# An S4D scan gated by an MLP: kernel tables through DRAM, outer products placed at once

## The chip, the core and the metric

The kernel runs on one core of one Trainium2 chip. The core has five engines with queues of their own: TensorE (matmuls; PE in the profile, its weight loads PEld), VectorE (DVE), ScalarE (ACT), GpSimd (POOL) and SyncE (SP), which here only issues DMAs. The metric is device time in microseconds: the median of three timed runs, and for the profile the span of one execution from its first to its last instruction.

## The reference

The input `A_u` is one sequence of 2048 tokens with 576 channels. It is layer-normalised, and the result goes two ways: through a long convolution per channel (S4D) and through an MLP whose SiLU gates the convolution.

```python
def _A_ref(u, log_A_real, A_imag, C_real, C_imag, log_dt, D_skip):
    ...
    P = jnp.exp((A * dt[:, None])[:, :, None] * pos[None, None, :])
    K = 2.0 * jnp.einsum("dn,dnl->dl", C, P).real
    ...
    Kf = jnp.fft.rfft(K, L2)
    Uf = jnp.fft.rfft(u_t, L2)
    y = jnp.fft.irfft(Uf * Kf[None, :, :], L2)[:, :, :L]
    ...
    return y + u * D_skip[None, None, :]

def _B_ref(x, w1, b1, w2, b2):
    y = _layernorm(x, axis=-1)
    h = _gelu(jnp.einsum("bsd,df->bsf", y, w1) + b1)
    return jnp.einsum("bsf,fd->bsd", h, w2) + b2

x = A_u
xn = _layernorm(x, axis=-1)
s = _A_ref(xn, ...)
g = _silu(_B_ref(xn, ...))
return x + s * g
```

The state size N is 128, the hidden size 4608. The result is float32.

## The kernel before

**The MLP** is cut into 48 slots: two halves of the tokens, 12 groups of 384 hidden units in each, and two blocks of 512 tokens (`tb`) in each group. A slot has 11 positions: three units of the first layer (14 matmuls of 512 columns each, line 633) and eight units of the second (72 matmuls of 288 columns in all, line 707). Every float32 operand is split into a high and a low part, and three products of these parts are summed. ScalarE applies the GELU (671) and takes the high part (674), VectorE takes the low part (677) and adds the second layer's result (717). Weights are loaded into `raw` by SyncE (551, 553) and split by ScalarE (586) and VectorE (583).

**The tables and outer products.** The convolution kernel of 16 channels (a block `b`, 36 of them) is a product of two small tables of complex powers. `tables(b)` makes them: `load_par` (944) fetches 30 numbers per channel and state, on GpSimd's queue, into one of two `par` buffers; VectorE makes the phases (963, 966, 972), ScalarE the integer parts and the sines (969, 975, 980, 982); VectorE makes the magnitudes `mg` (988) and the four products with the sines (997 to 1003). `kgen(b)` is the outer product: 64 small matmuls (1042), after which ScalarE copies the result into a tile `kt` (1047), one tile for 48 channels, two buffers.

**The chunks.** The convolution itself is a Fourier transform in two stages, made by matmuls, for six chunks of 96 channels. A chunk's steps on TensorE are X1 (1157, two, the signal's first stage), K1 (1188, two, the kernel's), S2 (1217, four, second stage of both), the inverse (1260, two) and I1 (1286, one). Between them ScalarE and VectorE split operands (1133, 1136), transpose (1165, 1196, 1271), multiply (1234) and add (1240). The matrix of the first stage, `f1t`, is split anew for each chunk (1111, 1114) into the buffer of the second stage's matrix, `f2t`.

**What sets the order.** A planner written in Python (`Order`) walks through the 48 slots with assumed durations and writes each engine's instructions in one fixed order. It keeps a clock per engine, a number of lines of steps (each line in order, lines earlier in its list first where two could start at once), and marks for what is done. MLP work is urgent and has due times; the rest fills what is left. DMA loads are steps without an engine, written into their queue when their conditions are met by the plan. After each position of a slot `pe_turns` may put a step of a chunk or an outer product between the MLP's matmuls; at 7 of the 11 positions chunk steps and outer products are allowed. `END` sets the pace of the chunk steps, `ALONE` how long a ready outer product waits for one. `ride` lets an outer product that is ready go inside a chunk step's place, using a free part of its accumulator. All chunk steps take both `cv` accumulators, an outer product alone takes one. `HOLD` moves some named VectorE steps behind the next one on their engine.

The second half's MLP inputs are stored to `y_s`, and before slot 24 loaded (486), transposed (491) and split (495 to 503) through the `row` buffers, of which there are four. The result is put together by `combine` (746 to 758, three `row` buffers per set) and, for the last eight token blocks, by `finish` (802 to 826).

Of the kernel before, what the change touches and what calls it, by code (L numbers as in the profile page):

```python
# [18 lines left out]
P = 128  # L19
# [9 lines left out]
E1, E8, E64, E512 = 2, 10, 18, 26  # L29
NPAR = 30  # L30
PK = 144
NXC, NROW = 1, 4
G = 3
NG = F // (P * G)
KB = 4
# [12 lines left out]
def pool(n):  # L48
    return 0.25 + 0.0023 * n

# [174 lines left out]
def mixer_kernel(ctx, tc, u, log_a_real, a_imag, c_real, c_imag, log_dt, d_skip, w1, b1, w2, b2,  # L225
# [24 lines left out]
    par_s = dr.tile([P, D, NPAR], F32, name="par_s")  # L250

# [13 lines left out]
    f1t = sb.tile([P, 2, 2, 64], F32, name="f1t")  # L265
# [34 lines left out]
    def odd_rows(part):  # L300
# [14 lines left out]
        if part == 1:  # L315
            for g in range(4):
# [86 lines left out]
    def norms(b0, n):  # L403
# [49 lines left out]
        def second(t):  # L453
            mv, rs = MV[b0]
            y = sb.tile([P, D], F32, name="row", bufs=NROW)
# [333 lines left out]
    def finish(b, c0, c1, silu, second_queue, z=None, store=(0, 0), flush=False,  # L789
# [7 lines left out]
        def act_z():  # L797
            if n < D:
                T.append(sb.tile([P, TB], F32, name="h32", bufs=2)[:, :n])
            else:  # L800
                T.append(sb.tile([P, D], F32, name="row", bufs=NROW))
# [33 lines left out]
    def params():  # L835
# [9 lines left out]
        PRM = [flat(sb.tile([P, 12, 64], F32, name="kt", bufs=2)) for _ in range(2)]  # L845
# [57 lines left out]
        add("DVE", d, lambda: V.scalar_tensor_tensor(cr, cr, 2.0, dt, op0=OP.mult, op1=OP.mult), mark="polar")  # L903
        early.append(step("DVE", d, lambda: V.tensor_mul(nrm, nrm, dt), need=["nrm"]))
# [5 lines left out]
        def pack(i):  # L910
            s = slice(i * PK, (i + 1) * PK)

            def columns():
                if i == 0:
                    V.memset(pt[:, :, E1:E1 + 17:8], 1.0)
                V.tensor_copy(pt[:, :, 0], th[:, s])
                V.tensor_copy(pt[:, :, 1], ph[:, s])
# [11 lines left out]
            early.append(step("DVE", 0.6 if i else 1.1, columns, need=["polar"]))  # L929
# [7 lines left out]
    PAR, TAB = {}, {}  # L937

    def load_par(b):
        if b == NB:  # L940
            return
# [11 lines left out]
    def tables(b):  # L953
# [5 lines left out]
        def phase(k):  # L959
            if k == 0:  # L960
                T["v"] = table_tile()
                T["w"] = T["v"][:, :, :, 32:]
                nc.vector.tensor_mul(T["w"][:, 1], bc(PAR[b][:, :, 0], 2, NV), bc(tv, 1, SB))
            else:
                u = T["w"][:, 1, :, 33:]
                nc.vector.tensor_add(u, u, bc(PAR[b][:, :, 1], 2, 32))
# [24 lines left out]
        def weigh(part):  # L991
# [10 lines left out]
            else:  # L1002
# [5 lines left out]
        return ([step(None, 10.0 if b < 6 else 4.5, lambda: load_par(b), mark=("par", b), need=[("pack", b * SB // PK)]  # L1008
                      + ([("mags", b - 2)] if b > 1 else [("xn", k) for k in range(8, NT)])),
                 step("DVE", dve(SB * NV), f(phase, 0), need=[("kg", b - 2)] if b > 1 else []),  # L1010
                 step("DVE", dve(n), f(phase, 1), hold=HOLD.get(("phase", b), 0)), step("ACT", act(SB * NV), whole),
                 step("DVE", dve(SB * NV), frac, hold=HOLD.get(("frac", b), 0)), step("ACT", act(SB * NV), fold, mark=("fold", b))],
                [step("ACT", act(SB * NV), f(sin, 0), need=[("fold", b)], mark=("sin", b, 0), tbl="sin"),
                 step("ACT", act(SB * NV), f(sin, 1), mark=("sin", b, 1), tbl="sin")],
                [step("DVE", dve(2 * n), f(mags, 0), need=[("par", b)]),
                 step("DVE", dve(n), f(mags, 1), mark=("mags", b))]
                + [step("DVE", dve((2, 2, 1, 1)[part] * n), f(weigh, part), need=[("sin", b, 1)],
                        mark=("wu", b) if part == 3 else None, hold=HOLD.get(("weigh", b, part), 0)) for part in range(4)])
# [10 lines left out]
    def kgen(b):  # L1029
# [3 lines left out]
        def mm(tile=None):  # L1033
            U, v = TAB[b]
            if r % 48 == 0:
                KT[c, r // 48] = sb.tile([P, 12, 64], F32, name="kt", bufs=2)
# [780 lines left out]
```

## Time and profile before

| what | number |
|---|---|
| timed runs, median (lowest to highest) | 1095.79 us (1095.51 to 1096.2) |
| the profiled execution's own time: its span | 1094.6 us |
| TensorE busy | 1087.5 us (99%) |
| VectorE busy | 891.6 us (81%) |
| ScalarE busy | 727.4 us (66%) |
| GpSimd busy | 188.3 us (17%) |
| DMA, mean over the span | 126 GB/s |
| TensorE's granted clock | 0.999 |

A page row of a group reads: line, engine, operation, tiles (written <- read), shapes and count, then busy time, the mean duration of one in ns, and the idle time of the engine just before them. A row of the timeline reads: start, duration, engine, line, operation, tiles, shape, count of merged instructions. A row of the waits reads: who waited <- for whom: total us, times, longest. Since matmuls overlap, a matmul's duration is longer than its step from start to start; the steps are what adds up.

### The profile page before, as it was taken

The numbers are of one execution on the slowest core, as the hardware profiler recorded it, in microseconds if no ns is written. First come the engines' busy times: TensorE is split into PE (matmuls) and PEld (weight loads), VectorE is DVE, ScalarE is ACT, GpSimd is POOL, SyncE is SP. The second block draws the span as 40 slices with busy tenths as digits, with TensorE's granted clock in tenths as the row PEclk, the third lists the DMA queues.
The fourth block names the chain that finished last, engine by engine and source line by source line (L and its number), as shares of the span: only waits on it lengthen the run. The fifth ranks groups of instructions, "written<-read, shape, count | busy, mean of one in ns | idle before, by whom it ended". The sixth has DMA issues, their size and how long they took to land.

```text
span 1094.6 us, 27052 instructions
## 1 busy us (share of the span) xinstructions
PE 1087.5 (99%) x11445; PEld 954.1 (87%) x11445; DVE 891.6 (81%) x1302; ACT 727.4 (66%) x1113; POOL 188.3 (17%) x261
## 2 busy tenths in 40 slices
PE   9999999999999999999999999999999999999998
PEld 7989899899888898888988888888888888888897
DVE  7698667889998879889899987997979888766367
ACT  6585699778676674777767848685675757534333
POOL 4566210153010100001100000000001021101132
PEclk9999999999999999999999999999999999999999
DMA  8846663626354152355624216133152434455454
GB/s 226 241 141 160 227 240 137 181 78 156 120 161 139 44 112 66 91 111 147 166 47 119 78 56 141 34 122 87 54 126 44 143 101 132 116 168 151 136 151 102
DMA packets 139554, 138.22 MB, mean 126 GB/s; under 512 B 88953, under 2 KB 105017, under 8 KB 138857
## 3 DMA queue, kind: packets, MB, share of 16 engines
q1 hardware_dynamic: 124424, 85.05, 29.4%
q0 software_dynamic: 14528, 50.71, 15.1%
q8 instruction: 89, 1.46, 0.6%
q10 hardware_dynamic: 480, 0.74, 0.3%
q14 instruction: 33, 0.26, 0.1%
HBM read 102.17 MB, written 36.63 MB: 127 GB/s over the span
## 4 chain that ended last, share of the span: by engine, by line
PE 95%; DMA 2%; DVE 1%; SPq 1%; issue 0%; ACT 0%; DVEq 0%
PE mxb L707 20%; PE mxa L707 20%; PE mxa L633 20%; PE mxb L633 20%; PE cv L1042 3%; PE cv L1217 3%; PE cv L1260 2%; PE cv L1286 2%; PE cv L1188 1%; PE cv L1157 1%; SPq L856 1%; DMA w<-in_A_u_dram 1%; DMA acc<-in_A_u_dram 0%; DMA h<-in_B_b_dram 0%; DVE st L423 0%; DMA raw<-in_B_w_dram 0%
## 5 line engine op out<-in xcount | busy, mean ns | idle before, releaser
L677 DVE TENSOR_TENSOR hl<-h,hh 128x512 fp32r<-128x512 f32 x144 | 98.4, 686 | 96.4 <-ACT hh L674 95.4
L707 PE MATMUL mxa<-w2h,hh 128*128 128x288 f32 x573 | 170.3, 297 | 0.0
L707 PE MATMUL mxb<-w2h,hh 128*128 128x288 f32 x573 | 170.2, 297 | 0.0
L707 PE MATMUL mxb<-w2h,hl 128*128 128x288 f32 x573 | 169.3, 296 | 0.2 <-DVE hl L677 0.2
L707 PE MATMUL mxa<-w2h,hl 128*128 128x288 f32 x573 | 169.1, 295 | 0.0
L707 PE MATMUL mxa<-w2l,hh 128*128 128x288 f32 x573 | 168.6, 294 | 0.0
L707 PE MATMUL mxb<-w2l,hh 128*128 128x288 f32 x573 | 168.6, 294 | 0.0
L671 ACT ACTIVATE h<-mxa,b1t 128x512 f32<-128x512 f32 x73 | 50.0, 687 | 99.2 <-PE mxa L633 97.8
L707 PEld LDWEIGHTS mxa<-w2h,hh 128*128 128x128 f32 x573 | 107.6, 188 | 5.9 <-issue 3.0
L707 PEld LDWEIGHTS mxb<-w2h,hh 128*128 128x128 f32 x573 | 107.6, 188 | 4.3 <-issue 1.7
L707 PEld LDWEIGHTS mxb<-w2l,hh 128*128 128x128 f32 x573 | 107.6, 188 | 0.8
L707 PEld LDWEIGHTS mxa<-w2l,hh 128*128 128x128 f32 x573 | 107.6, 188 | 0.6
L707 PEld LDWEIGHTS mxb<-w2h,hl 128*128 128x128 f32 x573 | 107.5, 188 | 0.5 <-DVE hl L677 0.4
L707 PEld LDWEIGHTS mxa<-w2h,hl 128*128 128x128 f32 x573 | 107.5, 188 | 0.0
L671 ACT ACTIVATE h<-mxb,b1t 128x512 f32<-128x512 f32 x71 | 48.8, 687 | 68.6 <-PE mxb L633 66.2
L674 ACT ACTIVATE hh<-h 128x512 fp32r<-128x512 f32 x144 | 90.7, 631 | 3.7
L944 POOL DMA_DIRECT2D par<-par_s x36 | 27.8, 773 | 367.8 <-DVE mg L988 324.8
L717 DVE TENSOR_TENSOR acc<-mxa,acc 128x576 f32<-128x576 f32 x87 | 65.4, 752 | 26.4 <-PE mxa L707 26.1
L717 DVE TENSOR_TENSOR acc<-mxb,acc 128x576 f32<-128x576 f32 (+1 forms) x89 | 65.8, 741 | 17.8 <-PE mxb L707 17.6
L633 PE MATMUL mxa<-XH,w1h 128*128 128x512 f32 x284 | 79.4, 401 | 0.0
L633 PE MATMUL mxb<-XH,w1h 128*128 128x512 f32 x280 | 77.6, 399 | 0.0
L633 PE MATMUL mxa<-XL,w1h 128*128 128x512 f32 x284 | 76.2, 390 | 0.0
(277 smaller groups left out, 2494.0 us busy)
## 6 DMA issues: line engine op xcount, KB each, us to landing
raw<-in_B_w_dram SPq DMA_DIRECT2D x72, 288.0 KB, 3.4
raw<-in_B_w_dram SPq DMA_DIRECT2D x96, 192.0 KB, 3.6
par_s<-A POOLq DMA_DIRECT2D x4, 2160.0 KB, 8.1
par<-par_s POOLq DMA_DIRECT2D x36, 240.0 KB, 3.7
f2t<-f2q SPq DMA_DIRECT2D x24, 256.0 KB, 3.7
g2t<-g2p SPq DMA_DIRECT2D x24, 256.0 KB, 4.3
bias<-XR SPq DMA_DIRECT2D x42, 128.0 KB, 3.6
raw<-in_B_w_dram SPq DMA_DIRECT2D x48, 96.0 KB, 3.8
```

The lines of the kernel that those rows point to most:

```text
L633: nc.tensor.matmul(q, a, b, start=j == 0 and i not in BEGUN, stop=j == len(ops) - 1, skip_group_check=True)
L671: nc.scalar.activation(t, q, AF.Gelu_apprx_tanh, bias=b1t[:, k:k + 1], scale=1.0)
L674: LAST[0] = nc.scalar.activation(hh[:, i], t, AF.Copy)
L677: nc.vector.tensor_sub(hl[:, i], t, hh[:, i].bitcast(F32))
L707: nc.tensor.matmul(q[:, dh, :288], a[:, i, c], b[:, i, d], start=i == 0 and k == 0 and alone != 1, stop=i == G - 1 and k == 2, skip_group_ ...
L717: nc.vector.tensor_add(o, q[:, dh:dh + n, :288], b)
L856: nc.sync.dma_start(r[32 * g:32 * g + 32].rearrange("c (b n) -> c b n", n=32), dram(src[k], 32 * g, [[N, 32], [32 * N, D // 32], [1, 32]]))
L944: nc.gpsimd.dma_start(PAR[b].rearrange("p (g i) k -> p g (i k)", g=4), dram(par_s, (b // 3 * 48 + b % 3 * 4) * NPAR, [[D * NPAR, P], [12 * ...
L1042: nc.tensor.matmul(q[32 * g:32 * g + 32, i // 2, i % 2 * 64:i % 2 * 64 + 64], U[:, ri, 4 * g + i, :], v[:, ri, 4 * g + i, :], start=ri == ...
L1217: nc.tensor.matmul(Q[i][32 * q:32 * q + 32, f, ri::2], m[r, 4 * i + q, 32 * ri:32 * ri + 32], A2[r, 4 * p + 2 * i + q // 2, :, :, q % 2], ...
L1260: nc.tensor.matmul(QI[q // 2][64 * f:64 * f + 64, q % 2, i], MAT["g2t", p + i // 2][r, i % 2, f, ri], YS[p + i // 2][0][r, i % 2, ri, f], ...
L1286: nc.tensor.matmul(Q[h][64 * y:64 * y + 64, t], g1t.rearrange("p a e -> p (a e)"), A2[:, k:k + 2, 1].rearrange("p i d r -> p i r d"), star ...
```

## The change

- The turns (the first two of the 30 numbers per channel and state) get a small DRAM table `turn_s` and a small tile `pa` with loads of their own, on SyncE's queue; the other 28 numbers stay in `par`, now one buffer, loaded by SyncE instead of GpSimd.
- An outer product's result goes through a small tile `ko` to a DRAM table `kt_s`; a chunk fetches its 48 channels from there into `kl`.
- The first transform's matrix is split once, into a tile `fp` that stays.
- The steps of tables and chunks are cut into more lines with other conditions: loads, phases, sines, magnitudes and products apart; signal parts, kernel parts and ScalarE's copies apart; the next chunk's signal parts may be made after the last kernel stage and inverse of the chunk before. Both sines are one step. `HOLD` is empty.
- An outer product that is ready goes at the next allowed place (`ALONE` 0, `DUE` gone); `END` goes from 1000 to 980.
- `row` has three buffers instead of four; some of its users move to the tile `xt`. The loads of the second half's inputs wait accordingly.

```diff
-E1, E8, E64, E512 = 2, 10, 18, 26
-NPAR = 30
+E1, E8, E64, E512 = 0, 8, 16, 24
+NPAR = 28
-NXC, NROW = 1, 4
+NXC, NROW = 1, 3
...
+    turn_s = dr.tile([P, 2, D], F32, name="turn_s")
+    kt_s = dr.tile([D // 48, P, 12, 64], F32, name="kt_s")
-    f1t = sb.tile([P, 2, 2, 64], F32, name="f1t")
+    FP = [sb.tile([P, 2, 2, 128], F32R, name="fp")]
...
+        def turns():
+            for k, t in enumerate((th, ph)):
+                nc.sync.dma_start(turn_s[:, k], t)
+        add(None, 7.0, turns, mark="pa")
...
-                V.tensor_copy(pt[:, :, 0], th[:, s])
-                V.tensor_copy(pt[:, :, 1], ph[:, s])
                 V.tensor_copy(pt[:, :, E512], cr[:, s])
...
+    def load_pa(b):
+        PA[b] = sb.tile([P, 2, SB], F32, name="pa", bufs=2)
+        nc.sync.dma_start(PA[b].rearrange("p v (g i) -> p v g i", g=4), dram(
+            turn_s, b // 3 * 48 + b % 3 * 4, [[2 * D, P], [D, 2], [12, 4], [1, 4]]))
     def load_par(b):
-        PAR[b] = sb.tile([P, SB, NPAR], F32, name="par", bufs=2)
-        nc.gpsimd.dma_start(PAR[b].rearrange("p (g i) k -> p g (i k)", g=4), dram(
+        PAR[b] = sb.tile([P, SB, NPAR], F32, name="par")
+        nc.sync.dma_start(PAR[b].rearrange("p (g i) k -> p g (i k)", g=4), dram(
...
+        return ([step(None, 4.5, lambda: load_pa(b), need=["pa"] + ([("phase", b - 2)] if b > 1 else []), mark=("pa", b))],
...
+                [step("ACT", 2 * act(SB * NV), lambda: (sin(0), sin(1)), need=[("fold", b)], mark=("sin", b), tbl="sin")],
+                [step(None, 10.0 if b < 6 else 5.0, lambda: load_par(b), need=[("pack", b * SB // PK)] + ([("mags", b - 1)] if b else []),
+                      mark=("par", b))],
+                [step("DVE", dve(2 * n), f(mags, 0), need=[("par", b)] + ([("wu", b - 1)] if b else [])),
...
         def out():
-            nc.scalar.activation(KT[c, r // 48][:, k0:k0 + SB // 4, :].rearrange("p (h i) m -> p h (i m)", h=2),
-                                 Q[0], AF.Copy)
-        need = [("kp", c - 1, r // 48)] if r % 48 == 0 and c else []
+            t = sb.tile([P, SB // 4, 64], F32, name="ko", bufs=2)
+            nc.scalar.activation(t.rearrange("p (h i) m -> p h (i m)", h=2), Q[0], AF.Copy)
+            nc.sync.dma_start(kt_s[b // 3, :, k0:k0 + SB // 4, :], t)
+        need = []
...
+            def fetch():
+                KT[c, i] = sb.tile([P, 12, 64], F32, name="kl")
+                nc.sync.dma_start(KT[c, i], kt_s[2 * c + i])
...
-            four.append(step("ACT", act(256), high, need=[("s2", c - 1, 3)] if c else ["odd", ("f2s", 7)]))
-            four.append(step("DVE", dve(256), low, mark=("fp", c)))
+            four.append(step("ACT", act(256), high, need=["odd"]))
+            four.append(step("DVE", dve(256), low, mark="fp"))
...
-        if c:
-            four.append(step(None, 5.0, lambda: None, need=[("st", c - 1)]))
-        f1_parts()
+        if not c:
+            f1_parts()
...
+            at = lambda w, k: [M(w, k)] if k >= 0 else [("turn", 0, 8, w, KB + 1 + k)] if tb else []
+            ml["steps"].append(step(None, 6.5, load, need=at("t", kb - 1) + at("l", kb - 2), mark=M("s", kb)))
+            mlt["steps"].append(step("DVE", dve(TB) + 0.05, turn, need=[M("s", kb)], mark=M("t", kb)))
...
-    END = 1000.0
+    END = 980.0
-    ALONE, DUE = 20.0, (160.0, 950.0)
+    ALONE = 0
...
-                    wait = ("wu", b + 1) not in od.marks or od.t["PE"] < DUE[0] + b * (DUE[1] - DUE[0]) / NB
-                    if b < NB - 1 and od.t["PE"] < h[1] + (ALONE if wait else 3.0):
+                    if b < NB - 1 and od.t["PE"] < h[1] + ALONE:
                         break
```

More of the change, by code (lines that the diff above doesn't have):

```diff
@@ L928, in pack @@
                                   need=() if i else [("xn", b) for b in range(4, 8)]))
-            early.append(step("DVE", 0.6 if i else 1.1, columns, need=["polar"]))
+            early.append(step("DVE", 0.25 if i else 0.8, columns, need=["polar"]))
             early.append(step("DVE", 0.65, rest))
@@ L1072, in mixer_kernel @@
     X1, S2, INV, I1, KG = 1.5, 1.75, 2.15, 3.05, 1.03
-    HOLD = {("weigh", 19, 3): 1, ("phase", 19): 1, ("frac", 18): 2, ("k", 2, 1): (2, 1), (2, 0, 24): 1, (2, 1, 24): 1, ("k1", 2, 1, 2): 1}
+    HOLD, KX = {}, 0
     def chunk(c):
         XC, MAT, YS = {}, {}, {}
-        one, two, three, four = [], [], [], []
+        one, two, three, four, five, six = [], [], [], [], [], []
         line = [one]
@@ L1314, in chunk @@
         i1()
-        return one, two, three, four
+        return one, two, three, four, five, six
     NPOS = G + 8
```

99 lines of the change are left out of this document (47 added, 52 removed).

## The prediction

> **What bounds the kernel now.** I read first the page's busy times and its chain, then the list of waits on TensorE, then the busy times by stage, and last the timeline of TensorE around single steps.
>
> ```profile
> span 1094.6 us, 27052 instructions
> PE 1087.5 (99%) x11445; PEld 954.1 (87%) x11445; DVE 891.6 (81%) x1302; ACT 727.4 (66%) x1113; POOL 188.3 (17%) x261
> ...
> PE 95%; DMA 2%; DVE 1%; SPq 1%; issue 0%; ACT 0%; DVEq 0%
> ```
>
> A busy TensorE may still be a stalled one, since the ends of matmuls are modelled. Two views settle it. The waits of TensorE:
>
> ```profile
> PE mxa L1348 <- POOL XL L1341: 1.3, 1, 1.3
> PE mxa L648 <- ACT XH L520: 0.4, 1, 0.4
> PE mxb L707 <- DVE hl L677: 0.2, 1, 0.2
> ```
>
> That is all: 1.9 us in 1094.6, and 1.7 of it in the warm-up (L1348) and at the first layer's first matmuls (L648). The other view is the timeline, where the starts count and not the durations. An outer product (L1042) that stands alone between two first-layer groups, and the last two matmuls of all:
>
> ```profile
> 193.21 1.07 PE L633 MATMUL mxb<-XL,w1h 128*128 128x512 f32 x4
> 194.12 1.07 PE L633 MATMUL mxb<-XH,w1l 128*128 128x512 f32 x4
> 195.25 0.39 PE L633 MATMUL mxb<-XR,w1s 128*128 128x512 f32 x1
> 195.57 1.11 PE L1042 MATMUL cv<-w 128*32 128x64 f32 x64
> 196.61 1.18 PE L633 MATMUL mxa<-XH,w1h 128*128 128x512 f32 x4
> ...
> 1088.99 0.30 PE L707 MATMUL cv<-w2l,hh 128*128 128x288 f32 x1
> 1089.13 0.29 PE L707 MATMUL cv<-w2h,hl 128*128 128x288 f32 x1
> ```
>
> Four first-layer matmuls start every 194.12 - 193.21 = 0.91 us, so one costs 0.2275. Second-layer ones (L707) start 1089.13 - 1088.99, about 0.13 to 0.14, apart. So TensorE is a stream of matmuls laid end to end, and the time is the sum of their spacings plus what follows the last one: 1094.6 - 1089.4 = 5.2 us.
>
> The change can therefore gain only by giving TensorE less to do, and lose by giving it more or by making it wait. It removes no matmul. What it alters is the places at which the side work (tables, outer products, chunk steps) is put into the stream, so the price of a place is the first term.
>
> **Term 1: outer products that go at once.** Read the quoted stretch again. From the last first-layer matmul (195.25) to the next group (196.61) are 1.36 us; less that matmul's own 0.23 leaves 1.13; and the next four take 1.18 where four elsewhere take 1.07, another 0.11. One outer product alone costs 1.24. Now one that shares its place with a chunk step (S2, L1217), and S2 without it:
>
> ```profile
> 580.23 0.39 PE L633 MATMUL mxb<-XR,w1s 128*128 128x512 f32 x1
> 580.54 1.10 PE L1042 MATMUL cv<-w 128*32 128x64 f32 x64
> 581.58 1.60 PE L1217 MATMUL cv<-A,f2t 64*32 64x192 f32 x64
> 583.11 1.20 PE L633 MATMUL mxa<-XH,w1h 128*128 128x512 f32 x4
> ...
> 727.77 0.39 PE L633 MATMUL mxa<-XR,w1s 128*128 128x512 f32 x1
> 728.09 1.62 PE L1217 MATMUL cv<-A,f2t 64*32 64x192 f32 x64
> 729.64 1.20 PE L633 MATMUL mxb<-XH,w1h 128*128 128x512 f32 x4
> ```
>
> Together 583.11 - 580.23 - 0.23 + 0.13 = 2.78; S2 alone 729.64 - 727.77 - 0.23 + 0.13 = 1.77. The shared outer product costs 1.01. So leaving and re-entering the stream once more costs 1.24 - 1.01 = **0.23 us**.
>
> How many now? The kernel has 36 outer products:
>
> ```profile
> L1042 PE MATMUL cv<-w 128*32 128x64 f32 x2304 | 39.7, 220 | 0.0
> ...
> 175.25 1.10 PE L1042 MATMUL cv<-w 128*32 128x64 f32 x64
> ...
> 646.28 1.10 PE L1042 MATMUL cv<-w 128*32 128x64 f32 x64
> ```
>
> (2304 / 64 = 36.) On the timeline 8 of them have MLP matmuls on both sides, the first at 175.25 and the last at 646.28, five of them before the first chunk step; 28 share a place. They share because the old rule lets a ready outer product wait 20 us (ALONE) for a chunk step to carry it. The new rule lets it go at the next allowed place. Two cases show what that does:
>
> ```profile
> 608.32 0.69 DVE L1003 SCALAR_TENSOR_TENSOR w<-w,mg 128x512 f32<-128x512 f32 x1
> ...
> 610.43 1.10 PE L1042 MATMUL cv<-w 128*32 128x64 f32 x64
> ...
> 508.64 0.69 DVE L1003 SCALAR_TENSOR_TENSOR w<-w,mg 128x512 f32<-128x512 f32 x1
> ...
> 531.03 1.10 PE L1042 MATMUL cv<-w 128*32 128x64 f32 x64
> ```
>
> L1003 is the last table product. The one of 608.32 was followed by a shared outer product at the very next place (610.43, an S2 right behind it); the one of 508.64 by one at 531.03, 22 us later. I went through the 31 that come after the first chunk step: in 14 the next allowed place already holds a chunk step, so they would share under the new rule too; in 17 they would go alone. Were the coincidence pure chance it would be rarer: 54 steps that can carry one (all but the 12 inverse ones), over 36 slots of 7 allowed places, is about one in five, or 25 alone. Against that, a step that holds both convolution banks keeps a single outer product out. I take 17, the count from this schedule: 5 + 17 = 22 alone, 14 more than now, 14 x 0.23 = **+3.2 us**. Bounds: all 36 alone, 28 x 0.23 = +6.4; none alone, 8 x 0.23 = -1.8.
>
> **Term 2: work off TensorE.** Two of three column copies per parameter piece go (eight of about 0.3 us, as L918) and five of six splits of the first transform's matrix:
>
> ```profile
> L918 DVE COPY A<-xc x4: 299/304/330, 108.6 to 185.5; 128x144 f32<-128x144 f32 x4
> ...
> L1111 ACT ACTIVATE f2t<-f1t x6: 400/405/409, 235.0 to 925.3; 128x256 fp32r<-128x256 f32 x6
> L1114 DVE TENSOR_TENSOR f2t<-f1t,f2t x6: 415/422/427, 236.8 to 926.1; 128x256 fp32r<-128x256 f32 x6
> ```
>
> That is 2.4 + 2.1 = 4.5 us of VectorE and 2.0 of ScalarE. TensorE waits for neither (0.6 us in all above), so it is worth **0**. Of the stretches of 50 us this is VectorE's fullest, and TensorE did not stand in it:
>
> ```profile
> 550.00:600.00 50.00, 50.00 (x616) 43.74 (x615) 48.24 (x65) 34.94 (x50) 3.33 (x4) 1.00 0.35 89
> ```
>
> (columns: TensorE, weight loads, VectorE, ScalarE, GpSimd). The tables no longer wait for the two table buffers of a chunk, so they will run ahead and fill VectorE earlier; at 48.2 of 50 there are 1.8 us of reserve per 50 us. A wholly full VectorE costs 0 as long as the planner keeps the hidden-layer and accumulator steps first, which it did here; if that cover fails, it is the second rival's kind of loss.
>
> **Term 3: DMA issues.** GpSimd loses 36 parameter loads. SyncE gains these, 36 small loads of the turns (two numbers per channel, 16-byte pieces), 36 stores and 12 loads of the kernel table and two stores: 122 issues. The nearest rows:
>
> ```profile
> raw<-in_B_w_dram SPq DMA_DIRECT2D x96, 192.0 KB, 3.6
> ...
> par<-par_s POOLq DMA_DIRECT2D x36, 240.0 KB, 3.7
> ...
> L1089 SPq DMA_DIRECT2D xc<-xn_s x48: 303/565/6048, 186.8 to 932.0; - x48
> ```
>
> The xc load, in 96-byte pieces, issues in 565 ns (the middle one of its three numbers), so 122 cost some 70 us of a queue that has time: between its issues it stands waiting for VectorE to free a buffer,
>
> ```profile
> SPq L551 <- DVE w1l L583: 259.3, 27, 27.8
> ```
>
> but it is one queue in order, and the weights (raw) travel on it. A parameter load that waits for the previous products (one buffer where there were two) holds up every weight load behind it. The planner writes each load where it thinks its buffer is free, so I take 0; bounds 0 (the landing of 3.6 us stays inside the lead) to one landing per pair of slots for a third of the 24 weight groups, 8 x 3.6 = 29, which I think far off; a quarter of that, +7, is the rival's price.
>
> [...]
>
> **Term 4: one row buffer fewer.** The loads of the second half's inputs (L486) now follow one another. Now they end early:
>
> ```profile
> L486 SPq DMA_DIRECT2D row<-y_s x36: 303/488/1587, 470.3 to 538.4; - x36
> ...
> row<-y_s SPq DMA_DIRECT2D x36, 64.0 KB, 2.9
> ...
> 528.37 0.69 DVE L501 TENSOR_TENSOR XL<-row,XH 128x512 fp32r<-128x512 f32 x1
> ...
> 545.14 0.68 DVE L503 TENSOR_TENSOR XR<-row,XR 64x512 fp32r<-64x512 f32 x1
> ...
> 556.87 0.39 PE L633 MATMUL mxa<-XR,w1r 128*128 128x512 f32 x1
> ```
>
> That leaves 11 us. A load is four issues of 0.49 and a landing of 2.9 us, 4.9; with its transpose 5.6. Three in a row after the first split of this half (529.1) end at 545.9, with the last one's own split near 548; two more of VectorE's queue per step give 554. Worth 0, bound +1.
>
> **Sum.** 1094.6 + 3.2 = 1097.8 of span; the runs' median, 1095.79, is 1.2 us above this span, so **1099.0 us**, 0.3% slower.
>
> **Rivals.** *The outer products share as before* (not slower): the place is the call that puts steps into the stream; chunk steps are asked first, and a ready outer product rides with them. If VectorE's order makes tables and chunk steps come ready together, as in the 14 cases, at most 10 more go alone, and the time is 1095.8 to 1098.0; with all riding 1094.0. For it: 14 of 31. Against: a chunk step that follows closer holds the banks longer, and tables that end early leave none to share with.
>
> *SyncE's queue holds up the weights*: a parameter load waits in front of a weight load, a split comes late, TensorE waits. For it: VectorE near full at 48.2 of 50, so plan and run drift. Against: no such wait now, though SyncE's queue waits for 259 us on one line alone. Price 3.2 + 7: near 1106, and 1102.5 with half of it.
>
> *The MLP's spacing itself shrinks* (faster): 1 ns less on 3456 second-layer matmuls is 3.5 us, 1092.3 without term 1. For it: other engines' accesses move. Against: no row quoted here shows a second-layer spacing that depends on what the others do.
>
> **How the numbers follow.** Forecast (10 or more extra alone, no stall) 0.43; sharing as before 0.31; weights late 0.16; spacing 0.10. With 0.2%, about what a measurement of this kernel can tell from no change, the bounds are 1093.6 and 1098.0: slower 0.43 + 0.16 = 0.59, same 0.31, faster 0.10. Range 1094.0 to 1104.0: all 36 alone is 1102.2; it leaves out the third rival and the upper half of the second.
>
> **What would show it.** Outer products alone on the timeline: near 22 says term 1, 8 to 18 the first rival; each at 1.24 against 1.01. The list of TensorE's waits should stay under 3 us; rows there naming ScalarE's or VectorE's weight splits are the second rival. L1111 x1 in place of x6 says the split was dropped. I am wrong if the number of lone outer products rises and the time does not, or if TensorE waits more than it gains in places.

## The result and the profile after

The changed kernel takes 1127.0 us (median of four runs, 1125.9 to 1127.6) against 1096.0 us of the kernel before on the same chip: ratio 1.0282, 95% interval 1.0268 to 1.0297. It is slower by 31 us; 3.2 had been forecast. The profiled execution spans 1124.1 us, 29.5 more than the one of before. From the page of the changed kernel (the lines compared here are 9 to 18 higher now: 716 was 707, 686 was 677, 1054 was 1042):

```profile
span 1124.1 us, 27216 instructions
PE 1097.0 (98%) x11445; PEld 955.3 (85%) x11445; DVE 888.9 (79%) x1289; ACT 713.2 (63%) x1099; POOL 160.7 (14%) x225
...
PE 80%; DVE 8%; DMA 6%; ACT 2%; POOL 2%; issue 1%; SPq 1%; ACTq 0%; DVEq 0%; POOLq 0%
```

The waits of TensorE in it:

```profile
PE mxb L716 <- DVE hl L686: 7.6, 1, 7.6
PE mxa L716 <- DVE hl L686: 4.4, 2, 3.4
PE mxa L1366 <- POOL XL L1359: 1.3, 1, 1.3
PE mxa L642 <- DVE XR L512: 0.9, 1, 0.9
PE mxa L642 <- ACT h L680: 0.8, 1, 0.8
PE mxa L642 <- DVE acc L726: 0.8, 1, 0.8
```

The number of matmuls is the same (x11445). New are TensorE's waits, nearly all for VectorE, and VectorE is less busy than before (888.9 against 891.6 us). So VectorE isn't short of time in sum; it is late at places. The chain of what ended last now runs 8% over VectorE and 6% over DMAs.

The largest wait on the timeline of the changed kernel, VectorE first and then TensorE:

```profile
116.05 0.69 DVE L686 TENSOR_TENSOR hl<-h,hh 128x512 fp32r<-128x512 f32 x1 [3.82 <-ACT hh L683]
127.34 1.24 DVE L977 TENSOR_TENSOR w<-pa,tv 128x1040 f32<-128x1040 f32 x1 [10.60 <-DMA kk<-turns_s]
128.50 0.68 DVE L686 TENSOR_TENSOR hl<-h,hh 128x512 fp32r<-128x512 f32 x1
...
121.20 0.29 PE L716 MATMUL mxb<-w2h,hh 128*128 128x288 f32 x1
121.33 0.29 PE L716 MATMUL mxb<-w2l,hh 128*128 128x288 f32 x1
129.24 0.61 PE L716 MATMUL mxb<-w2h,hl 128*128 128x288 f32 x1 [7.62 <-DVE hl L686]
129.64 0.44 PE L716 MATMUL mxb<-w2h,hh 128*128 128x288 f32 x1
129.88 0.44 PE L716 MATMUL mxb<-w2l,hh 128*128 128x288 f32 x1
```

TensorE idles for 7.6 us; by the steps from start to start the wait costs 129.24 - 121.33 - 0.13 = 7.8. VectorE does nothing for 10.6 us, because in its written order the first table step (L977) stands ahead of the low part `hl` (L686) that TensorE needs. L977 reads `pa`. The profile names another transfer that landed at about the same time (`kk<-turns_s`, which L977 doesn't read); the landing of `pa` itself shows whose fault it was. The issues on SyncE's and GpSimd's queues, on the timeline of the changed kernel:

```profile
109.00 0.68 SPq L952 DMA_DIRECT2D pa<-turn_s  x1
...
109.16 0.59 POOL L942 DMA_DIRECT2D par_s<-A  x1 [2.22 <-DVE A L936]
109.74 1.97 POOL L346 DMA_DIRECT2D f2p<-in_f_dram  x4
```

And the DMA rows: the landing of this load alone, and the shortest, middle and longest landing of all 36.

```profile
pa<-turn_s SPq DMA_DIRECT2D x1, 16.0 KB, 18.2
...
DMA to landing us min/median/max: 2.5/2.8/18.2
```

Issued at 109.0 and landed 18.2 us later, where the plan allowed 4.5 and such a load otherwise takes 2.8 (the median). GpSimd's queue moved 2016 KB and four times 512 KB in the same stretch.

The second wait is of the same kind: chunk 0's kernel rows, planned at 5 us, issued at 274.58, and VectorE stands before them until 280.7. TensorE's 3.40 us are 3.6 from start to start:

```profile
274.58 0.53 SPq L1187 DMA_DIRECT2D kl<-kt_s  x1
...
280.72 0.18 DVE L1190 TENSOR_TENSOR kl<-kl,dsk 128x12 f32<-128x12 f32 x1 [2.98 <-DMA kl<-kt_s]
...
282.71 0.61 PE L716 MATMUL mxa<-w2h,hl 128*128 128x288 f32 x1 [3.40 <-DVE hl L686]
```

After each of the two waits TensorE is slow for a while. In the rows above, the second-layer matmuls after 129.64 start every 0.24 us and before the wait every 0.13. Busy times by stretch of the changed kernel (TensorE, weight loads, VectorE, ScalarE, GpSimd, then the granted clock, the DMA engines' share, GB/s):

```profile
110.00:121.00 11.00, 11.00 (x55) 9.35 (x55) 1.45 (x2) 2.65 (x4) 4.46 (x9) 1.00 1.04 379
121.00:127.00 6.00, 0.62 (x5) 0.39 (x3) 0.00 (x0) 5.93 (x13) 1.16 (x2) 0.87 0.64 54
127.00:134.00 7.00, 4.76 (x26) 4.76 (x27) 5.06 (x8) 5.43 (x20) 0.00 (x0) 0.63 0.60 160
```

The granted clock is half (0.50) for 6.83 us around the first wait, from 125.4 to 132.2, and for 3.41 us around the second, from 282.4 to 285.9:

```profile
125.41:132.23 6.82, 2.99 (x12) 2.99 (x13) 4.45 (x7) 6.81 (x25) 0.00 (x0) 0.50 0.64 133
...
282.43:285.85 3.42, 3.14 (x13) 3.15 (x14) 3.42 (x5) 3.39 (x4) 1.61 (x3) 0.50 0.97 360
```

Some 13 matmuls pay 0.11 us each time, 1.4 us. What sets the two lengths isn't shown.

The end of the changed kernel: the last matmul on the timeline, and by line (shortest, middle and longest duration in ns, first and last start in us) the last step of the closing combine and its stores; then that step of the combine in the kernel before.

```profile
1114.55 0.29 PE L716 MATMUL cv<-w2h,hl 128*128 128x288 f32 x1
...
L764 DVE TENSOR_TENSOR row<-row x11: 557/559/758, 920.7 to 1112.9; 128x384 f32<-128x384 f32 x9, 128x576 f32<-128x576 f32 x2
...
L767 POOL DMA_DIRECT2D out_dram<-row x32: 527/531/562, 921.6 to 1115.3; - x32
```

```profile
L755 DVE TENSOR_TENSOR row<-row x11: 557/558/758, 876.7 to 1078.8; 128x384 f32<-128x384 f32 x9, 128x576 f32<-128x576 f32 x2
```

9.3 us follow the last matmul, 5.2 before. The combine is 11 sets one after another, (1112.9 - 920.7) / 10 = 19 us apart; it enters the plan at slot 38, and its first set comes 44 us later now. So does the slot: by the count of second-layer matmuls on the timeline, slot 38 starts at 920.9 us instead of 875.0, 46 us later, while the last matmul is only 25 us later.

So the 29.5 us are, by the traces: TensorE's waits over 0.3 us, the warm-up's 1.3 aside, 16.4 against 0.4, that is 16.0; half clock after two of them 2.8; 28 lone outer products (alone between two groups of MLP matmuls) in place of 8, 20 x 0.23 = 4.6; the end 4.1; 2.0 not placed.

### The profile page after: what moved, and what is told of

The parts are those of the page before. It is cut to its first block, busy times and chain, and to the rows that moved or that the text cites. A ratio compares the mean times of both kernels' runs of the same rounds, so it can differ in the third digit from the quotient of the medians.

```text
span 1124.1 us, 27216 instructions
## 1 busy us (share of the span) xinstructions
PE 1097.0 (98%) x11445; PEld 955.3 (85%) x11445; DVE 888.9 (79%) x1289; ACT 713.2 (63%) x1099; POOL 160.7 (14%) x225
## 4 chain that ended last, share of the span: by engine, by line
PE 80%; DVE 8%; DMA 6%; ACT 2%; POOL 2%; issue 1%; SPq 1%; ACTq 0%; DVEq 0%; POOLq 0%
PE mxb L716 17%; PE mxa L716 17%; PE mxa L642 16%; PE mxb L642 16%; PE cv L1233 3%; PE cv L1054 3%; PE cv L1279 2%; PE cv L1305 2%; PE cv L1170 1%; PE cv L1207 1%; DMA raw<-in_B_w_dram 1%; DMA f2p<-in_f_dram 1%; DVE hl L686 1%; DMA kk<-turns_s 1%; DVE acc L726 1%
## 5 line engine op out<-in xcount | busy, mean ns | idle before, releaser
L686 DVE TENSOR_TENSOR hl<-h,hh 128x512 fp32r<-128x512 f32 x144 | 98.6, 687 | 114.8 <-ACT hh L683 114.1
L595 ACT ACTIVATE w2h<-raw 128x576 fp32r<-128x576 f32 x72 | 44.6, 676 | 54.2 <-PE mxa L716 53.0
```

Of the source, the lines that this page charges most:

```text
L595: nc.scalar.activation(h, r, AF.Copy)
L686: nc.vector.tensor_sub(hl[:, i], t, hh[:, i].bitcast(F32))
```

## The experiments

All are compared with the kernel before on the same chip, which took 1095.3 to 1096.0 us in each group of runs. The counts of lone outer products in the experiments are those of the plan; the timelines show up to two more (26 where 25 is said, 9 where 7 is said).

### The first load of the turns

```diff
-        return ([step(None, 4.5, lambda: load_pa(b), ...
+        return ([step(None, 20.0 if b < 2 else 4.5, lambda: load_pa(b), ...
```

> The changed kernel, but the plan gives the first two loads of the turns 20 us instead of 4.5, so VectorE's first phase stands later in its order; the loads themselves are the same. If VectorE stood behind the first 16-byte load and held the hidden layer's low parts (7.8 us of TensorE, and 1.4 us of half clock after it), the stall at 121 us goes and the time is 1127.0 - 9.2 = 1117.8 us; three more outer products stand alone (31), +0.7, so near 1118.5. If VectorE waited there for something else, the stall stays and the time is near 1127.

Measured 1114.3 us (1112.4 to 1118.5), 12.7 less, more than expected. The load still took 18.3 us, and nobody stood before it. The second wait shrank too: two of 1.4 and 1.2 us in place of 3.4, and the mean granted clock of the profiled execution is 0.998 instead of 0.993.

The pieces of the load, regrouped in DRAM so that it is 128 pieces of 128 bytes (the six copies that do this stand in lines not shown):

```diff
...
-        nc.sync.dma_start(PA[b].rearrange("p v (g i) -> p v g i", g=4), dram(
-            turn_s, b // 3 * 48 + b % 3 * 4, [[2 * D, P], [D, 2], [12, 4], [1, 4]]))
+        nc.sync.dma_start(PA[b].rearrange("p v i -> p (v i)"), dram(
+            turn_s, b * 32, [[2 * D, P], [1, 32]]))
```

> The changed kernel, with the turns put into the order of the blocks by six small VectorE copies before they are stored, so that a load is 128 pieces of 128 bytes instead of 1024 of 16. TensorE's order stays that of the changed kernel (28 outer products alone). If the many small pieces make the first load slow, it lands in under 6 us instead of 18.2 and the stall at 121 us shrinks below 2 us: near 1118 us. If the DMA engines are simply full at that time (2 MB of parameters on GpSimd's queue), it still lands after more than 12 us, and the time is near 1127.

Measured 1119.6 us (1119.0 to 1119.9), between the two expectations. The first landing fell from 18.2 to 10.6 us, TensorE's wait from 7.6 to 4.2, and the median landing from 2.8 to 1.9. But the copies also put the load 6.1 us later, at 115.07 in place of 109.00, and it landed at 125.7 in place of 127.2, so this run doesn't show how much of the fall the pieces made. It shows that larger pieces alone don't take the load past the bulk (10.6 us beside it, 1.9 the median); how the small pieces go beside it is seen in the next section.

### The queue of the parameter loads

```diff
-        nc.sync.dma_start(PAR[b].rearrange("p (g i) k -> p g (i k)", g=4), dram(
+        nc.gpsimd.dma_start(PAR[b].rearrange("p (g i) k -> p g (i k)", g=4), dram(
```

> The changed kernel with the 36 parameter loads (L958) put back on GpSimd's queue, where the kernel before has them; all else as changed. Theory (the two long stalls are the first turn load and chunk 0's kernel rows, not these loads, and SyncE's extra issues cost nothing themselves): between 1123 and 1131. Rival (the added issues on SyncE's queue are the cause, as my prediction's second rival had it): 1115 or less.

Measured 1117.0 us, but in two groups: 1111.7, 1112.4, 1121.6 and 1122.5. Both expectations missed. In the profiled execution (1112.4) the wait at 121 us isn't there: the first load landed after 2.6 us. What the landing goes with is seen when its issue is set against the issue of the 2016 KB store on GpSimd's queue, over all kernels of this study with the 16-byte pieces (from the same two kinds of rows as above):

| load issued ahead of the store by, us | 0.91 | 0.85 | 0.53 | 0.45 | 0.39 | 0.38 | 0.26 | 0.17 | 0.16 | 0.01 | -0.11 | -0.66 |
|---|---|---|---|---|---|---|---|---|---|---|---|---|
| landing, us | 2.6 | 2.6 | 2.7 | 7.9 | 16.5 | 17.9 | 18.3 | 18.8 | 18.2 | 18.2 | 18.0 | 17.3 |

Two of these, each with the issues from the timeline and the landing from the DMA rows: this run's kernel, and then the one with four kinds of loads planned late (below).

```profile
109.35 0.68 SPq L952 DMA_DIRECT2D pa<-turn_s  x1
...
110.20 0.59 POOL L942 DMA_DIRECT2D par_s<-A  x1 [3.14 <-DVE A L936]
...
pa<-turn_s SPq DMA_DIRECT2D x1, 16.0 KB, 2.6
```

```profile
108.68 0.68 SPq L952 DMA_DIRECT2D pa<-turn_s  x1
...
109.21 0.59 POOL L942 DMA_DIRECT2D par_s<-A  x1 [3.32 <-DVE A L936]
...
pa<-turn_s SPq DMA_DIRECT2D x1, 16.0 KB, 2.7
```

In these twelve traces a lead of half a microsecond over the bulk parts landings of 3 us from those of 18. The changed kernel has 0.16. In this run's own trace the second turn load, issued 0.6 us after the store, took 18.5 us.

The packets show how. By queue (packets, MB, share of the 16 DMA engines' time; q0 carries GpSimd's transfers, as its 4.19 MB show: 2016 KB, four times 512 and 32; q1 SyncE's, as the number of its pieces shows), in the changed kernel from 110 to 123 us and from 123 to 128 us, and then in the kernel with all loads planned late and the rule (below) from 109 to 111 us:

```profile
q0 software_dynamic: 292, 4.19, 99.3%
q1 hardware_dynamic: 278, 0.00, 1.2%
...
q1 hardware_dynamic: 2393, 0.38, 50.3%
```

```profile
q1 hardware_dynamic: 1040, 0.02, 28.4%
```

The first two turn loads of the changed kernel are 2048 pieces. While the bulk runs, 278 of them go in 13 us, 21 a microsecond; the other 1770 follow from 123 to 128 us. Where the load is ahead of the bulk, its 1024 pieces go within 2 us. So the pieces are slow beside the bulk and fast ahead of it; what their number adds beside it isn't shown.

This run, and the ones with the earlier end and with the old pace in the changed kernel, show two groups of times 6 to 10 us apart, and their profiled executions fit the race: those of the faster groups have the load landed in 2.6 and 7.9 us, one of a slower group in 16.5. Each kernel has one trace, so that the race parts the other executions isn't shown. On the question asked, whether the parameter loads on SyncE cost anything themselves, this run says nothing: the race of the two queues covers it.

### The end

```diff
-    later(NSLOT - 10, 4, end_line)
+    later(NSLOT - 13, 4, end_line)
```

> The changed kernel with one number altered: the closing combine chain (L763, L764, and its loads and stores) enters the plan at slot 35 instead of slot 38; nothing on TensorE is meant to move. Theory (the chain is 11 sets one after another, about 19 us each, and hung on a slot that now comes late; it alone sets what follows the last matmul): the time behind the last matmul falls from 9.3 us to about 5, TensorE's stream keeps its 1113 us, so 1123 us. Rival (the tail is set by the last chunk's products, which the chain waits for): tail and time stay, 1127.

Measured 1117.8 us (1114.0, 1114.9, 1120.6, 1121.4). In the profiled execution (1121.4) 5.6 us follow the last matmul instead of 9.3; the wait at 121 us is 5.6 instead of 7.6. The end is what was expected. The rest of the gain goes with that load, which landed after 16.5 us in this trace; for the two executions near 1114 us, which have no trace, the load is the likely cause and not shown.

### Three numbers at once

```diff
-        return ([step(None, 4.5, lambda: load_pa(b), ...
+        return ([step(None, 20.0 if b < 2 else 4.5, lambda: load_pa(b), ...
-            kfl["steps"].append(step(None, 5.0, fetch, ...
+            kfl["steps"].append(step(None, 5.0 if c else 14.0, fetch, ...
-    later(NSLOT - 10, 4, end_line)
+    later(NSLOT - 13, 4, end_line)
```

> The changed kernel with three numbers of the plan altered and no instruction: the first two turn loads are planned at 20 us, chunk 0's two fetches of kernel rows at 14 us instead of 5, and the combine chain enters at slot 35. 28 outer products stay lone. Theory (the slowdown is the sum of loads that land later than planned in front of a VectorE that works in a fixed order, of 20 more lone outer products at 0.23, and of the tail): 1127.0 less 7.8 + 1.4 for the first stall, 3.6 + 1.4 for the second and 4.2 for the tail, that is 1108.6; what is left over the kernel before is the lone products (4.6) and the small stalls (about 5). Rival (any shift of the plan only moves the stalls to other places): 1114 or more.

Measured 1110.7 us (1109.8 to 1111.4), ratio 1.0132 (1.0117 to 1.0147), near the sum and off the rival. 16.3 of the 31 us were three numbers of the plan; no instruction was changed, only their order.

### The at-once rule in the kernel before, and the pace

The rule alone in the kernel before, with the holds emptied (25 lone outer products instead of 8):

```diff
-    HOLD = {("weigh", 19, 3): 1, ("phase", 19): 1, ...}
+    HOLD = {}
-                    if b < NB - 1 and od.t["PE"] < h[1] + (ALONE if wait else 3.0):
+                    if b < NB - 1 and od.t["PE"] < h[1]:
```

> The kernel before, with the new rule alone: an outer product that is ready goes at the next allowed place, and no VectorE step is held back by name. 25 instead of 8 stand alone. By the price of 0.23 us a place: +3.9 us, 1099.8 us, and TensorE's waits stay under 3 us. If going at once by itself fills VectorE and makes TensorE wait, it is slower than 1105.

Measured 1124.2 us (1122.4 to 1125.7): as slow as the whole change, and far from 4 us. Its control, the holds alone:

```diff
-    HOLD = {("weigh", 19, 3): 1, ("phase", 19): 1, ...}
+    HOLD = {}
```

> The kernel before with its hand-set holds emptied, and nothing else: the outer products still wait for a first-layer place. It is the control for the kernel before with the at-once rule, which had the holds emptied too. Theory (the at-once rule made the slowdown there: lone products, a VectorE stall of 5.4 us at 484 us, a late last chunk): within 2 us of 1096, tail about 5 us, no stall over 1 us. Rival (the holds, which were set by hand for this plan, carried it): 1110 or more, with a tail above 10 us.

Measured 1097.4 us, ratio 1.0012 (1.0003 to 1.0021): the holds are worth 1.4 us. And the rule with the pace of the change:

```diff
 (as the rule alone, and)
-    END = 1000.0
+    END = 980.0
```

> The kernel before with the at-once rule and emptied holds, and the pace of the chunk steps set to end at 980 us instead of 1000 as the change does. There the last product I1 ended at 1069 us (1024 in the kernel before) and the stores behind it at 1122, 17 us after the last matmul. Theory (the tail is the closing combine, which waits for the last chunk; a tighter pace brings that forward by up to 20 us): the tail falls to 5 to 8 us and the time by about 10, to 1114. Rival (the chunk steps are late because their inputs are, not by the pace): tail above 14, 1122 or more.

Measured 1100.4 us (1100.1 to 1100.7): the tail fell as expected, the time by 24 us where 10 were expected. Its control, the pace alone:

```diff
-    END = 1000.0
+    END = 980.0
```

> The kernel before with the pace set to end at 980 us instead of 1000, and nothing else: outer products wait as they did and the holds stand (9 lone ones, 78 breaks of the stream). It is the control for the run with the at-once rule and 980, which took 1100.35. Theory (a lone outer product costs 0.23 us, and the at-once rule there cost 16 x 0.23 = 3.7 us and little more): within 1.5 us of 1096. Rival (the tighter pace by itself changes the time, by other stalls or by freeing the end): 1099 or more, or 1093 or less.

Measured 1096.7 us, ratio 1.0005 (0.9996 to 1.0015). The two runs at 980 give the price of the rule where nothing else goes wrong: 1100.35 - 1096.67 = 3.7 us for 25 lone outer products instead of 9, 16 x 0.23 = 3.7. They agree in size, no closer: the runs differ in the holds too, worth 1.4 us at the old pace, and ran on different chips, against whose kernels before the difference is 4.3.

At 1000, the rule makes a plan that fails. The last product of a chunk (L1286) and the last step of the combine (L755), by line, in the kernel at 1000 and then in the one at 980:

```profile
L1286 PE MATMUL cv<-A,g1t x96: 497/498/553, 370.6 to 1069.5; 128*64 128x384 f32 x96
...
L755 DVE TENSOR_TENSOR row<-row x11: 557/558/759, 890.9 to 1116.3; 128x384 f32<-128x384 f32 x9, 128x576 f32<-128x576 f32 x2
```

```profile
L1286 PE MATMUL cv<-A,g1t x96: 497/498/553, 361.1 to 1027.9; 128*64 128x384 f32 x96
...
L755 DVE TENSOR_TENSOR row<-row x11: 557/558/757, 883.6 to 1082.9; 128x384 f32<-128x384 f32 x9, 128x576 f32<-128x576 f32 x2
```

At 1000 the last chunk ends 42 us later, 16.8 us follow the last matmul, and there is a wait of 5.2 us at 484 us with second-layer matmuls every 0.24 us behind it instead of 0.13; at 980, 5.1 us and, behind the warm-up, no wait over 0.6. That the last chunk comes late whatever the pace is refuted; why 20 us of pace shift the chunk by 42 isn't shown.

The changed kernel with the pace of the kernel before:

```diff
-    END = 980.0
+    END = 1000.0
```

> The changed kernel with the pace of the kernel before, 1000 us instead of 980 (25 lone outer products, 96 breaks). Theory (the stalls at 121 and 279 us and the tail come of the turn loads, the kernel rows and the closing chain, not of the pace): within 4 us of 1127. Rival (the pace decides, as it did in the kernel before with the at-once rule, 1124 against 1100): 1135 or more, or 1115 or less.

Measured 1115.1 us, again in two groups (1112.7, 1114.3, 1116.0 and 1124.7). The profiled execution is of the first, its load landing after 7.9 us. It lies outside the theory's 4 us and at the rival's edge, and the race of the load covers it: this run doesn't tell what the pace does in the changed kernel.

The old rule in the changed kernel (14 lone):

```diff
-    ALONE = 0
+    ALONE, DUE = 20.0, (160.0, 950.0)
...
```

> The changed kernel with the old rule for a ready outer product (wait up to 20 us, or 3 us when it is due). 14 instead of 28 stand alone. By the price of 0.23 us of a place: 14 x 0.23 = 3.2 us less, 1123.8 us, the stalls unchanged. If the old rule also held the tables back so that VectorE is less full between 250 and 800 us, the small stalls (5 us) shrink too: near 1119. If outer products that wait delay chunk steps, no gain: 1127.

Measured 1118.2 us with a wide scatter (1114.9 to 1126.5). In the profiled execution (span 1124.7) TensorE waits for VectorE's `hl` five times, 14.0 us in all: 7.5 at 123 us, and at 503 us 2.0, while VectorE stands 4.4 before a load of the second half's inputs. The gain in places is lost among such waits; inconclusive for the rule.

With the three numbers and a wait of at most 10 us (8 lone):

```diff
 (as the three numbers, and)
-    ALONE = 0
+    ALONE = 10
```

> The same three altered numbers as in the run with three, and the outer products may wait up to 10 us for a place beside other side work: 8 lone ones instead of 28. Theory (lone products at 0.23 us each): 20 x 0.23 = 4.6 us less than the run with three, so 1104. Rival (the re-shuffled order meets other late loads): no gain over the run with three, or a loss, with VectorE waiting for a load ahead of TensorE's wait.

Measured 1104.8 us (1103.4 to 1106.9), 5.9 less than with the three numbers alone, 4.6 expected.

### What is left: loads that land late

Two more numbers of the plan:

```diff
 (as the last one, and)
-            ml["steps"].append(step(None, 6.5, load, need=at(...
+            ml["steps"].append(step(None, 12.0, load, need=at(...
-                [step(None, 10.0 if b < 6 else 5.0, lambda: load_par(b), need=...
+                [step(None, 16.0 if b < 6 else 5.0, lambda: load_par(b), need=...
```

> The run with four altered numbers, and two more: the row loads of the second half's inputs are planned at 12 us instead of 6.5, the first six parameter loads at 16 instead of 10. No instruction changes. Theory (each long wait of TensorE is VectorE standing in its fixed order before a load that lands later than planned; plan that load later and other work is put ahead of it): the waits at 287 us (2.8) and at 485 and 489 us (1.6 and 1.9) go, so 1104.75 less about 6, near 1099, with 2 us or less of long stalls left. Rival (VectorE is simply too full; stalls move elsewhere): 1103 or more, with stalls of as much in sum.

Measured 1101.3 us (1100.9 to 1101.7), ratio 1.0052 (1.0037 to 1.0067), nearer to the theory's 1099 than to the rival's 1103. The waits at 287, 485 and 489 us are gone; 3.4 us of others are left, the warm-up's 1.3 aside; the largest waits of TensorE in it:

```profile
PE mxa L716 <- DVE hl L686: 2.5, 2, 1.6
PE mxa L1366 <- POOL XL L1359: 1.3, 1, 1.3
PE mxa L657 <- ACT XH L529: 0.4, 1, 0.4
```

It has 7 lone outer products and keeps all of the change's tables and buffers. So in this plan the change's tables, queues and buffers, with what the plan still loses, cost 5.7 us together; the rest was landing times in the plan, the rule and the place of the end. No version run here beats the kernel before; of those with the change's tables this one comes nearest.

The same with the change's own rule (27 lone), and with a wait of 15 us and the old pace (6 lone):

```diff
-    ALONE = 10
+    ALONE = 0
```

> The same late planning of all four kinds of loads and the earlier combine chain, with the change's own rule that outer products go at once (27 lone ones instead of 7). Theory: 20 x 0.23 = 4.6 us more than the run with waiting up to 10 us, so about 1104. Rival (the price of going at once is more than the lone places, as 5.9 us between the two earlier runs hints): 1106 or more.

Measured 1109.0 us, 7.7 more than the last: the rival's side. TensorE's waits, the warm-up's aside, are 5.8 us instead of 3.4, so 5.3 are left for 20 places, 4.6 by the price.

```diff
-    ALONE = 10
+    ALONE = 15
-    END = 980.0
+    END = 1000.0
```

> All loads planned late, the earlier combine chain, outer products that may wait up to 15 us, and the pace of the chunk steps as in the kernel before: 6 lone outer products and 76 breaks of the stream, as many as before has. Theory: 1 to 2 us less than the run with 10 us, 1097 to 1098, at best the time of before; the change has nothing to win, since TensorE's work is the same. Rival (VectorE's lighter load pays off once the stalls are gone): below 1095.

Measured 1117.3 us: both expectations missed by 20 us, though it has the fewest lone outer products. The waits are 11.9 us, against 3.4 in the run with a wait of 10 us; a lower granted clock (0.991 in the mean of the profiled execution against 0.999) and a tail of 8.7 us instead of 5.7 come on top. The largest wait is at 475 us, where VectorE stands before the first row load although it was planned at 12 us. VectorE and SyncE's queue in it:

```profile
470.37 1.02 DVE L592 TENSOR_TENSOR w1l<-raw,w1h 128x384 fp32r<-128x384 f32 x2
477.77 0.71 DVE L500 STREAM_TRANSPOSE row<-row 128x512 f32<-128x512 f32 x1 [6.38 <-DMA row<-y_s]
...
466.18 0.38 SPq L958 DMA_DIRECT2D par<-par_s  x1
471.00 0.33 SPq L1110 DMA_DIRECT2D f2t<-f2q  x1
471.42 0.39 SPq L560 DMA_DIRECT2D raw<-in_B_w_dram  x1
471.90 1.98 SPq L495 DMA_DIRECT2D row<-y_s  x4
```

The load wasn't slow: it went out at 471.9, after VectorE had begun to stand. Ahead of it on SyncE's queue is an `f2t` load that waits 4.4 us for the matmuls that still read its buffer. The kernel before with the rule shows the same at 484 us. Planning its row loads at 12 us:

```diff
 (the rule alone in the kernel before, and)
-            ml["steps"].append(step(None, 6.5, load, need=last("t"), mark=M("s", kb)))
+            ml["steps"].append(step(None, 12.0, load, need=last("t"), mark=M("s", kb)))
```

> The kernel before with the at-once rule and emptied holds, and the row loads of the second half's inputs planned at 12 us instead of 6.5. Theory (its stall of 5.4 us at 484 us with the half clock behind it is VectorE standing before such a load, 5.06 us idle): that stall goes, 1124.2 less 5.4 less 1.4, about 1117.5; the tail of 17 us stays. Rival (the stall comes of a full VectorE): 1122 or more.

Measured 1129.9 us, 5.7 more: the wait stays (5.1 us, VectorE standing 5.4 before the load), others are added. The number in the plan didn't help here. To see whether the held queue is why, the first two row loads were moved to ScalarE's queue, in both kernels:

```diff
-                nc.sync.dma_start(T[0][32 * g:32 * g + 32]...
+                (nc.scalar if tb == 0 and kb < 2 else nc.sync).dma_start(T[0][32 * g:32 * g + 32]...
```

> The run with all loads planned late and a wait of 15 us, with one thing altered: the eight issues of the first two row loads (L495) go out from ScalarE's queue instead of SyncE's. In that run SyncE stood 4.4 us at an f2t load (L1110) that waits for S2's matmuls, and the row loads behind it went out at 471.9; VectorE then sat idle 6.4 us for them and TensorE 5.75 us. Theory (SyncE's queue, in order, holds up the row loads behind a load that waits for its buffer): the stall at 475 goes with the half clock behind it, 1117.3 less 5.8 less 1.4, about 1110. Rival (the load itself is slow, or VectorE is just too full): 1116 or more, with VectorE still idle over 4 us before L500.

Measured 1117.2 us (1113.5 to 1117.8), as before the move. Its profiled execution is the fastest one (1113.5; the others took 1116.8 or more) and has the wait at 3.2 us instead of 5.6, VectorE standing 4.0.

> The kernel before with the at-once rule and emptied holds, the same eight issues moved from SyncE's to ScalarE's queue. There SyncE stood 8.3 us at such an f2t load (L1097) and the row loads went out at 479.5 (470.3 in the kernel before); VectorE sat idle 5.1 us for them. Theory (SyncE's queue): the stall of 5.4 at 484 and its half clock go, 1124.2 less 6.8, about 1117.5, with the tail of 17 us as it was. Rival: 1123 or more.

Measured 1123.7 us; the wait is 4.0 instead of 5.2 us. The load's issues moved forward by 1.5 and 1.0 us in the two traces, and the wait shrank by 2.4 and 1.2, so SyncE's queue is part of it. The times are the rival's all the same (1116 and 1123 or more): the medians moved by 0.1 and 0.4 us, and in both ScalarE now stands behind the row loads' issues, 6.2 and 3.9 us, which may take back what the move gained. Most of the wait stays; the load is put too late into either queue, and why is open.

## Why the prediction was wrong, point by point

- **What bounds the kernel** was read rightly: TensorE's stream, end to end. That TensorE waits for nothing is a property of one order of instructions, and was taken for a reserve that any order has.
- **Term 1** holds in its price: leaving the stream once more costs 0.23 us, by the timeline and in size by the runs at 980. The count was too low: 28 alone instead of 22, since only 8 of 36 still found a chunk step at the next place; the bare chance named beside it (25 of 31, so 30 with the five before) was nearer. 4.6 us instead of 3.2. A lone one in the changed kernel, 0.23 off and 0.13 for the longer group after it: 162.92 - 161.57 - 0.23 + 0.13 = 1.25.

```profile
161.57 0.39 PE L642 MATMUL mxa<-XR,w1s 128*128 128x512 f32 x1
161.89 1.10 PE L1054 MATMUL cv<-w 128*32 128x64 f32 x64
162.92 1.20 PE L642 MATMUL mxb<-XH,w1h 128*128 128x512 f32 x4
```

- **Term 2** failed in its cover. "Costs 0 as long as the planner keeps the hidden-layer and accumulator steps first" looked at how full VectorE is. It does keep them first in the plan; on the chip a step whose load is late stands before them, and VectorE was idle, not full, in the two longest waits. The splits went as said (L1123 once).
- **Term 3** is the step that cost most. It sized the 122 issues by their time on the queue and by the middle landing of other loads (3.6 us), and took 0; its upper bound of 29 it called far off. What counted was one landing of 18.2 us and one of some 6 where the plan had 4.5 and 5: 7.8 + 3.6 of waits and 2.8 of half clock, 14 us. Its rival looked at the same queue and expected the weights to be held up; no row of TensorE's waits names a weight split. The landing of such a load, measured, is 2.8 us in the middle, 1.9 with 128-byte pieces, and 18.2 beside the bulk.
- **Term 4** (row buffers): a wait of 0.9 us at L512 is of the size of its bound; that the missing buffer made it isn't shown.
- **The end** had no term. Work that moves to earlier slots (the last X1 starts at 880 us instead of 943) makes those longer and the later ones shorter, so slot 38, on which the combine hangs, came 46 us later and the last matmul 25: 4.1 us.
- **The rivals.** Sharing as before didn't happen; the spacing didn't shrink (0.13 as before). The marker "TensorE's waits under 3 us" showed the failure at once.

## What to carry to other kernels

Where an engine works in one fixed order, each load ahead of a critical step is a wait in the making: list the new loads, and for each the transfers that are in flight when it is issued, and plan it by the worst landing in the trace, not by the median. That nothing waits holds for one order: here two small changes of it cost 0.7 and 1.4 us, and a third 28. So give a reordering a term for waits at its new loads, and look at what hangs on fixed places, such as the closing steps.

## What the runs showed of the hardware

In these traces a 16 KB load of 1024 pieces on SyncE's queue landed in 2.6 to 2.7 us when issued 0.53 to 0.91 us ahead of a 2016 KB store on GpSimd's queue with four loads of 512 KB behind it, in 7.9 when 0.45 ahead, and in 16.5 to 18.8 when issued from 0.39 us ahead to 0.66 after it; with eight times larger pieces, issued 3.6 us after the store, it took 10.6. While that bulk ran in the changed kernel, 21 of the small pieces went in a microsecond; where they were ahead of it, all 1024 went within 2 us. The granted clock of the changed kernel was half for 6.83 us around the wait of 7.6 us and for 3.41 us around that of 3.4; second-layer matmuls started every 0.24 us in these stretches instead of 0.13, which added 1.4 us each time. In the kernel before with the at-once rule they started every 0.24 us behind the wait of 5.2 us.
